# One VectorE order for another in a fused Fourier-filter and SoLU kernel: where two kinds of sums stand in the queue, and how one operand is laid out

## The chip, the cores and the metric

The kernel runs on one core of one Trainium2 chip. The time is device time of that core in microseconds, from one execution of the whole program. Seven executions of the kernel before gave a median of 1732.12 us (1724.58 to 1738.16).

## What is computed

The reference has two parts. The first filters a sequence in the frequency domain: eight examples of 3136 positions by 256 channels, a real Fourier transform along the positions, a product with a complex filter, and the transform back.

```python
X = np.fft.rfft(x, axis=1)
Y = X * (filt_r + 1j * filt_i)[None]
y = np.fft.irfft(Y, n=3136, axis=1)          # (8, 3136, 256)
```

The second takes the 25088 rows of that result through a two-layer block with a softmax-gated unit and a layer norm between the layers.

```python
h = x @ w_in                                  # 256 -> 1024
sm = softmax(h); solu = h * sm
ln = (solu - mean) / sqrt(var + 1e-6) * g_ln
out = ln @ w_out                              # 1024 -> 256
```

Everything is float32.

## The kernel before

**Blocks and pairs.** The 25088 tokens are 196 blocks of 128. A loop `step(k)` runs 205 times; block k's first layer is done in step k, its softmax and normalization in step k+2, its transpose in step k+3, and its second layer some nine steps after its first. Two steps, an even and an odd one, make a pair of blocks. Both layers use Strassen's scheme with seven products on 2x2 halves, so the unit of TensorE work is a pair: seven products of the first layer (line 716, `product(j, m)`, m from 1 to 7, 128x512 outputs) and seven of the second (line 828, `project(p, m)`, four 128x128 matmuls each, which the trace lists as eight instructions). The order of the products is 1, 2, 6, 7 in the even step and 5, 3, 4 in the odd step.

**Who empties the PSUM banks.** ScalarE copies a finished product out with `keep` (line 726) or `keep_out` (line 840, scaled). VectorE adds the later products to what was kept with `finish` (lines 737 and 740, which also find the running minimum for the softmax) and `finish_out` (line 844). Product 7 goes to a bank of its own. `finish(j, k, 1, (k - 1, 1), 2)` reads it, adds the half that was kept after product 5, and only then may product 4 add to the same bank. I call this `finish` the sum of product 7. In the same way project 7 may start only after `finish_out(p, 0, 0, ...)` in the odd step has read project 2, and the even step's `finish_out(p, 1, 0, ...)` needs project 4.

**The steps between.** `exponential` (line 748, ScalarE) and `normalize` (lines 759 to 766) do the softmax: two tiny VectorE instructions, a 128x1024 product with an accumulated mean on VectorE (line 764), and a square on ScalarE (line 766). `turn` (line 774) transposes a block of 128x1024 in 32x32 squares on VectorE. `regroup` (line 786) is the DMA, issued on SP, that brings the transposed squares into place, and `project_sums` (line 695) makes Strassen's sums on GpSimd.

**The Fourier part of the next example runs beside it.** While the blocks of example e are in the two layers, example e+1 or so goes through its transform: loads (line 240, SP), the difference and the sum of two quarters (line 249 VectorE, line 255 GpSimd), first step (line 264 TensorE, line 269 ScalarE), forward products (line 296), filter products (`multiply`, lines 317 to 319, VectorE, one half in the even step and one in the odd step after), the inverse (line 296 and ScalarE line 334). The last stage, the step back, is `back_halves`: 64 small matmuls (line 367) make an even and an odd half in two PSUM banks, ScalarE copies the even half to SBUF (line 371), and `join_halves` (lines 379 and 380, VectorE) adds and subtracts the halves into the tokens `y`, 128x392 elements each. A list `PLAN` gives the step of each piece by hand. The eight pieces of each of examples 2 to 7 fall in even steps; those of example 1 fall in steps 16 to 22, three of them odd and two in step 20.

**Order.** The whole loop is recorded under a manual schedule, so each engine's queue holds its instructions in the order in which `step` emits them, and each engine works its queue in order. Work of the Fourier part hangs in lists by step: `stores` at the start of a step, `products` after the odd step's sum of product 7, `early` behind the exponential, and `late` at the end of the step.

Of the kernel before, what the change touches and what calls it, by code (L numbers as in the profile page):

```python
# [23 lines left out]
N1, N2 = 49, 64  # L24
# [5 lines left out]
NCH = 4  # L30
KD, KF = C // P, DFF // P
PAIR = 2 * S
NT = PAIR // P
LAG = 9
# [60 lines left out]
def kernel(  # L95
# [10 lines left out]
    nc = tc.nc  # L106
# [247 lines left out]
    joins = {}  # L354

    def back_halves(e, ch, pss):

        t4 = t4s.pop((e, ch))
        views = [ps.rearrange("p a c -> p (a c)")[:, 0:KD * NCH * N1].rearrange(
            "p (c i r) -> p c i r", c=KD, i=NCH) for ps in pss]  # L360
        for cb in range(KD):
            for i in range(NCH):
                for g in range(2):
                    rows = slice(64 * g, 64 * g + NK // 2)
                    for h in range(2):
                        c0 = cb * P + 64 * h
                        nc.tensor.matmul(out=views[g][64 * h:64 * h + 64, cb, i, :],  # L367
                                         lhsT=t4[rows, i, c0:c0 + 64], rhs=wb_t[rows],
                                         start=True, stop=True)
        even = t4.rearrange("p i c -> p (i c)")[:, 0:KD * NCH * N1]  # L370
        nc.scalar.copy(out=even, in_=pss[0].rearrange("p a c -> p (a c)")[:, 0:KD * NCH * N1])
        joins[e, ch] = even.rearrange("p (c i r) -> p c i r", c=KD, i=NCH), views[1]

    def join_halves(e, ch):

        even, odd = (v.rearrange("p c i r -> p c r i") for v in joins.pop((e, ch)))
        t0, last = e % 2 * S, N2 // NCH - 1
        to = y[:, :, t0:t0 + S].rearrange("p c (r m j) -> p m c r j", m=N2 // NCH, j=NCH)
        nc.vector.tensor_tensor(out=to[:, ch], in0=even, in1=odd, op=ALU.add)
        nc.vector.tensor_tensor(out=to[:, last - ch], in0=even[:, :, :, ::-1], in1=odd[:, :, :, ::-1],  # L380
                                op=ALU.subtract)
# [14 lines left out]
    with ExitStack() as st:  # L396
# [154 lines left out]
        for n in range(16):  # L551
            (nc.sync, nc.scalar)[n % 2].dma_start(
                out=t2_0[NH * (n % 4):NH * (n % 4) + NH, n // 4, :], in_=rows_x[n:n + 1])
# [6 lines left out]
        for i in range(units):  # L560
# [4 lines left out]
            pss = [ps_t.tile([P, 2, C], FP32, name=f"pc_0_{i}_{u}", tag="t") for u in range(2)]  # L565
# [17 lines left out]
        for i0, n, rows in ((0, 4, P), (4, 4, P), (8, NP - 9, P), (NP - 1, 1, NQ)):  # L583
            f, at = filters[i0]
            nc.sync.dma_start(
                out=f_dram[i0:i0 + n].rearrange("i u q k c -> (u q) i (k c)")[0:rows],
                in_=f[0:rows, at:at + n].rearrange("p i k c -> p i (k c)"))
# [134 lines left out]
    def keep(j, k, i):  # L722

        if k not in hs:
            hs[k] = hpool.tile([P, DFF], FP32, name=f"h_{k}", tag=f"h{k % 2}")
        nc.scalar.copy(out=h_half(k, i), in_=ms[j, 0])  # L726

    def finish(j, k, i, kept, bank):


        if k not in nmaxs:
            nmaxs[k] = small.tile([P, 2], FP32, name=f"nmax_{k}", tag=f"nmax{k % 2}")
            sofar, to = 3.0e38, nmaxs[k][:, 0:1]
        else:
            sofar, to = nmaxs[k][:, 0:1], nmaxs[k][:, 1:2]
        if kept is None:
            nc.vector.tensor_scalar(out=h_half(k, i), in0=ms[j, bank], scalar1=0.0, scalar2=sofar,
                                    op0=ALU.add, op1=ALU.min, accum_out=to)
        else:
            nc.vector.tensor_tensor_reduce(out=h_half(k, i), in0=ms[j, bank], in1=h_half(*kept),  # L740
                                           scale=1.0, scalar=sofar, op0=ALU.add, op1=ALU.min,
                                           accum_out=to)
# [104 lines left out]
    def store_out(p):  # L847
# [7 lines left out]
    blocks = NT * B // 2  # L855

    early, late, stores, loads, products = (
        [[] for _ in range(blocks + LAG + 1)] for _ in range(5))  # L860

    def ahead(t, by):
        return loads[max(0, t - by)]
# [3 lines left out]
    for e in range(1, B):  # L867
        first_at, spectrum_at, back_at = PLAN[e]
        sp = Spectrum(e, pools, load_filter, load_de)
        if e == 1:  # L870
            sp = second
            sp.load, sp.load_de = load_filter, load_de
        for i, t in enumerate(first_at):
            dma = nc.gpsimd.dma_start
            if e == 1:
                if i not in sp.xs:
                    row_loads.append((t, t - 1, -1, lambda sp=sp, i=i, dma=dma: sp.fetch_x(i, [dma] * 2)))
                for u in range(2):
                    (early, late)[u][t].append(lambda sp=sp, i=i, u=u: sp.first(
                        i, (u,), psum(f"pa_{sp.e}_{i}_{u}").rearrange("p a c -> p (a c)").rearrange(  # L880
                            "p (o n) -> p o n", o=1), nc.scalar.copy, sp.xs[i][0:NK, 2 * u:2 * u + 2, :]))
                    (early, late)[u][t].append(lambda sp=sp, i=i, u=u: sp.store_first(
                        i, 2 * u, nc.gpsimd.dma_start))
            else:

                row_loads.append((t, t - 2, -1, lambda sp=sp, i=i: sp.fetch_quarters(i, nc.sync.dma_start)))
                stores[t].append(lambda sp=sp, i=i: sp.difference(i))
                products[t].append(lambda sp=sp, i=i: sp.sum(i))
                late[t].append(lambda sp=sp, i=i: sp.first_quarters(
                    i, [psum(f"pa_{sp.e}_{i}_{g}") for g in range(2)]))  # L890
                stores[t + 1].append(lambda sp=sp, i=i, dma=dma: sp.store_quarters(i, dma))
        for i, t in enumerate(spectrum_at):

            other = e == 1 and i % 2 == 1 and t + 1 < LAG
            add = nc.gpsimd.tensor_tensor if t + 1 < LAG else nc.vector.tensor_tensor


            dma = nc.sync.dma_start if e == 1 else nc.scalar.dma_start
            ahead(t, 2).append(lambda sp=sp, i=i, dma=dma: sp.fetch(i, dma))
            ahead(t, 1 if e == 1 and i % 2 == 1 else 2).append(lambda sp=sp, i=i: sp.fetch_filter(i))  # L900
            ahead(t, 2).append(lambda sp=sp, i=i: sp.fetch_de(i))
            early[t].append(lambda sp=sp, i=i, o=other: sp.forward(i, psum_pair(f"pb_{sp.e}_{i}", o)))
            late[t].append(lambda sp=sp, i=i, add=add: sp.multiply(i, 0, add))
            products[t + 1].append(lambda sp=sp, i=i, add=add: sp.multiply(i, 1, add))
            late[t + 1].append(lambda sp=sp, i=i, o=other: sp.inverse(i, psum_pair(f"pc_{sp.e}_{i}", o)))
            stores[t + 2].append(lambda sp=sp, i=i: sp.store(i, nc.gpsimd.dma_start))


        assert S * (e - 1) <= P * (back_at[0] // 2 * 2) and P * (back_at[-1] + 2) <= S * e // P // 2 * 2 * P
        for ch, t in enumerate(back_at):  # L910
            row_loads.append((
                t, t - 1, spectrum_at[-1] + 2, lambda e=e, ch=ch: fetch_back(e, ch)))
            (late if ch and t == back_at[ch - 1] else early)[t].append(lambda e=e, ch=ch: back_halves(
                e, ch, [psum(f"py_{e}_{ch}_{g}") for g in range(2)]))
            late[t].append(lambda e=e, ch=ch: join_halves(e, ch))
    row_loads.sort(key=lambda load: load[0])
    for n, (t, latest, earliest, load) in enumerate(row_loads):

# [10 lines left out]
    def step(k):  # L929
        j, odd = divmod(k, 2)  # L930
        p = j - (LAG - 1) // 2 if odd else j - (LAG + 1) // 2
        if not 0 <= p < pairs:
            p = None
# [5 lines left out]
        if not odd:  # L939
            if hid:  # L940
                product(j, 1)
                keep(j, k, 0)
            if proj:
                project(p, 5)
                keep_out(p, 1, (0, 1))
            if hid:
                product(j, 2)
        else:
            if hid:
                product(j, 5)  # L950
                keep(j, k - 1, 1)
        if 3 <= k < blocks + 3:
            turn(k - 3)
        if not odd and 0 <= j - 3 < pairs:
            regroup(j - 3, 0)
        if not odd:
            if proj:
                finish_out(p, 1, 1, (0, 1), 1)
            if hid:
                finish(j, k, 0, (k, 0), 1)  # L960
        elif hid:
            finish(j, k, 1, (k - 1, 1), 2)
        for job in products[k]:
            job()
        if 2 <= k < blocks + 2:
# [32 lines left out]
                project(p, 7)  # L998
        if 2 <= k < blocks + 2:
            normalize(k - 2)  # L1000
        if not odd:
            if proj:
                finish_out(p, 1, 0, (1, 0), 1)
                store_out(p)
        else:
            if hid:
                finish(j, k - 1, 1, None, 0)
                finish(j, k, 0, (k, 0), 2)
            if proj:
                keep_out(p, 1, (1, 0))  # L1010
# [39 lines left out]
```

## Time and profile before

| | |
|---|---|
| median of seven executions | 1732.12 us |
| the profiled execution, its own time | 1724.58 us |
| its span of instructions | 1722.8 us |
| TensorE busy | 1577.5 us (92%) |
| VectorE busy | 1298.1 us (75%) |
| GpSimd busy | 1122.8 us (65%) |
| ScalarE busy | 905.8 us (53%) |
| mean granted TensorE clock | 0.982 |

A busy share says how long an engine had an instruction in it, over stages of different kinds. What a change of order is worth is read from the waits: which engine stood idle, before which of its instructions, and whose work ended that idle time. The profile names for each idle stretch the instruction that released it. A line such as `m<-w_in_sb,y` names the tile written and the tiles read; `y` as an operand marks the products that take tokens directly (1, 2 and 4), `s` those that take sums (5, 6, 7 and 3). In timelines the columns are start, duration, engine, line, operation, tiles, shape and count, and in brackets the idle time before and what ended it.

### The profile page before, as it was taken

To read this page: it belongs to the slowest core of one execution; us is meant where nothing else is said; L and a number is where in the kernel's file an instruction comes from. 1 tells how busy PE (TensorE), PEld (TensorE's weight loads), DVE (VectorE), ACT (ScalarE), POOL (GpSimd) and SP (SyncE) were. 2 spreads that over 40 slices of the span, in tenths; PEclk is the share of its full clock that TensorE was granted. 3 is DMA by queue.
4 is the path that set the end of the run, shared out by engine and by line. 5 is a ranking of instruction groups with operands and counts; after the bars stand their busy time and mean duration, and the time that the engine had idled before them with its cause. 6 is when DMAs were issued, how large, how long until landed. Compare 5 with 4: busy or idle time off the path is not lost.

```text
span 1722.8 us, 36835 instructions
## 1 busy us (share of the span) xinstructions
PE 1577.5 (92%) x12710; PEld 1054.5 (61%) x12710; DVE 1298.1 (75%) x2633; ACT 905.8 (53%) x1772; POOL 1122.8 (65%) x1325
## 2 busy tenths in 40 slices
PE   5798789899988999899999998999999999999996
PEld 1353456666656666566656675566665777777776
DVE  1676787887777887787878778786788788777771
ACT  2154454456544555555455654555545656666662
POOL 4444785678666766677567865677655766666663
PEclk8999999999999999999999999999999999999998
DMA  9987888887888788867888778876786666555554
GB/s 254 254 263 212 238 207 208 206 200 178 182 214 216 178 187 220 216 159 167 209 206 202 178 168 214 204 178 162 182 208 146 134 128 126 115 107 107 110 109 91
DMA packets 377805, 312.13 MB, mean 181 GB/s; under 512 B 63322, under 2 KB 343395, under 8 KB 377619
## 3 DMA queue, kind: packets, MB, share of 16 engines
q1 hardware_dynamic: 306260, 169.81, 46.7%
q0 software_dynamic: 34464, 101.68, 20.8%
q10 hardware_dynamic: 36896, 38.28, 8.2%
q8 instruction: 103, 1.69, 0.4%
q14 instruction: 82, 0.67, 0.1%
HBM read 124.86 MB, written 81.50 MB: 120 GB/s over the span
## 4 chain that ended last, share of the span: by engine, by line
PE 54%; DMA 23%; DVE 10%; SPq 4%; POOL 3%; issue 3%; ACT 1%; ACTq 0%; DVEq 0%; POOLq 0%
PE o L828 23%; PE m L716 22%; DMA solu_t<-turn 10%; SPq L786 3%; PE py L367 3%; DMA x<-in_x_dram 2%; DVE turn L774 2%; DMA de<-de_tbl 2%; PE pb L296 2%; PE pa L264 2%; DVE h L764 2%; DMA rows<-rs 1%; PE pc L296 1%; DMA t<-d 1%; DMA out_dram<-ot 1%
## 5 line engine op out<-in xcount | busy, mean ns | idle before, releaser
L766 ACT ACTIVATE e<-h,nmu 128x1024 f32<-128x1024 f32 x196 | 224.8, 1147 | 398.9 <-DVE h L764 398.7
L828 PEld LDWEIGHTS o<-w_out_sb,solu_t 128*128 128x128 f32 x3136 | 384.6, 194 | 60.3 <-issue 37.8
L828 PE MATMUL o<-w_out_sb,solu_t 128*128 128x128 f32 x3136 | 405.3, 278 | 10.2 <-DVE rsum L759 7.4
L828 PEld LDWEIGHTS o<-w_out_sb,u 128*128 128x128 f32 x2352 | 313.2, 195 | 149.7 <-issue 116.9
L716 PE MATMUL m<-w_in_sb,s 128*128 128x512 f32 x784 | 396.3, 607 | 7.8 <-ACT h L726 5.0
L695 POOL TENSOR_TENSOR u<-solu_t 128x512 f32<-128x512 f32 x98 | 140.1, 1430 | 374.1 <-DMA solu_t<-turn 214.3
L716 PE MATMUL m<-w_in_sb,y 128*128 128x512 f32 x588 | 317.4, 623 | 64.4 <-DVE nmax L740 62.1
L828 PE MATMUL o<-w_out_sb,u 128*128 128x128 f32 x2352 | 318.9, 280 | 8.3 <-ACT ot L840 5.8
L844 DVE SCALAR_TENSOR_TENSOR ot<-o,rs_t,ot 128x128 f32<-128x128 f32 x294 | 102.5, 349 | 281.2 <-ACT ot L840 168.2
L764 DVE SCALAR_TENSOR_TENSOR h<-e,rsum,h 128x1024 f32<-128x1024 f32 x196 | 285.8, 1458 | 6.9
L726 ACT COPY h<-m 128x512 f32<-128x512 f32 x294 | 173.5, 590 | 204.2 <-PE m L716 190.8
L774 DVE STREAM_TRANSPOSE turn<-h 128x1024 f32<-128x1024 f32 x196 | 242.4, 1237 | 0.5
L748 ACT ACTIVATE e<-h,nmax 128x1024 f32<-128x1024 f32 x196 | 226.1, 1153 | 0.0
L716 PEld LDWEIGHTS m<-w_in_sb,y 128*128 128x128 f32 x588 | 93.5, 192 | 177.1 <-DVE nmax L740 131.6
L716 PEld LDWEIGHTS m<-w_in_sb,s 128*128 128x128 f32 x784 | 128.5, 191 | 95.7 <-issue 70.4
L840 ACT ACTIVATE ot<-o,rs_t 128x128 f32<-128x128 f32 x392 | 142.5, 363 | 74.2 <-PE o L828 65.9
L695 POOL TENSOR_TENSOR u<-solu_t,u 128x512 f32<-128x512 f32 x98 | 138.7, 1415 | 63.6 <-PE o L828 59.6
L740 DVE CUSTOM_DVE_ANT_0 h<-m,h 128x512 f32<-128x512 f32 x196 | 132.0, 673 | 37.9 <-ACT h L726 22.6
L695 POOL TENSOR_TENSOR u<-u,solu_t 128x512 f32<-128x512 f32 x98 | 139.0, 1419 | 0.6
L695 POOL TENSOR_TENSOR solu_t<-solu_t,solu_t 128x512 f32<-128x512 f32 x98 | 132.6, 1353 | 7.7
L695 POOL TENSOR_TENSOR s<-y 128x128 f32<-128x128 f32 x196 | 102.6, 524 | 1.7 <-DVE y L380 0.7
L367 PEld LDWEIGHTS py<-wb_t,t 50*64 50x64 f32 x3584 | 58.3, 134 | 44.5 <-PE o L828 14.4
(113 smaller groups left out, 1977.5 us busy)
## 6 DMA issues: line engine op xcount, KB each, us to landing
solu_t<-turn SPq DMA_DIRECT2D x784, 128.0 KB
out_dram<-ot SPq DMA_DIRECT2D x196, 128.0 KB
t<-d POOLq DMA_DIRECT2D x112, 200.0 KB, 4.7
d<-x POOLq DMA_DIRECT2D x100, 200.0 KB, 5.9
f<-f_dram POOLq DMA_DIRECT2D x39, 512.0 KB, 8.6
d<-g POOLq DMA_DIRECT2D x39, 512.0 KB, 5.1
t<-d ACTq DMA_DIRECT2D x36, 512.0 KB
x<-in_x_dram SPq DMA_DIRECT2D x112, 98.0 KB
```

The lines of the kernel that those rows point to most:

```text
L367: nc.tensor.matmul(out=views[g][64 * h:64 * h + 64, cb, i, :], lhsT=t4[rows, i, c0:c0 + 64], rhs=wb_t[rows], start=True, stop=True)
L695: nc.gpsimd.tensor_tensor(out=out, in0=in0, in1=in1, op=op)
L716: nc.tensor.matmul(out=ms[j, bank], lhsT=lhsT, rhs=w_in_sb[:, w, :], start=m in (1, 2, 7), stop=True, skip_group_check=True)
L726: nc.scalar.copy(out=h_half(k, i), in_=ms[j, 0])
L740: nc.vector.tensor_tensor_reduce(out=h_half(k, i), in0=ms[j, bank], in1=h_half(*kept), scale=1.0, scalar=sofar, op0=ALU.add, op1=ALU.min, ...
L748: nc.scalar.activation(out=e, in_=hs[k], func=AFT.Exp, bias=nmaxs.pop(k)[:, 1:2], scale=-1.0, accum_out=esum)
L764: nc.vector.scalar_tensor_tensor(out=solu, in0=e, scalar=rsum, in1=solu, op0=ALU.mult, op1=ALU.mult, accum_out=nmu)
L766: nc.scalar.activation(out=e, in_=solu, func=AFT.Square, bias=nmu, scale=-float(DFF), accum_out=variances[g][:, i:i + 1])
L774: nc.vector.transpose(out=turns[g][:, :, i, :], in_=solus.pop(k).rearrange("p (f j) -> p f j", j=32))
L828: nc.tensor.matmul(out=pos[p, bank], lhsT=lhs[:, f, :], rhs=w[:, f, :], start=f == 0 and m in (1, 2, 7), stop=True, skip_group_check=True)
L840: nc.scalar.activation(out=out_half(p, *to)[0], in_=pos[p, 0], func=AFT.Copy, scale=rs)
L844: nc.vector.scalar_tensor_tensor(out=ot, in0=pos[p, bank], scalar=rs, in1=out_half(p, *kept)[0], op0=ALU.mult, op1=ALU.add)
```

## The change

Three edits, all of them to work on VectorE and to one ScalarE copy. Neither the number of instructions of any kind nor the order on TensorE, ScalarE, GpSimd or SP is changed.

1. The joins of the step back move from the end of the step (`late`) to a new list `middle`, which is emitted directly behind `normalize`: ahead of the even step's last `finish_out`, and in an odd step ahead of its two last `finish`. A second step back in the same step (there is one) stays in `late`.
2. In odd steps the sum of product 7 is emitted ahead of `turn` where it was behind it.
3. The even half is written by the ScalarE copy in the order in which the join reads it (channel half, row, position in the group of four). The copy therefore reads PSUM with a step of 49 elements where it read it in sequence, and writes SBUF in sequence as before. The join reads this operand in sequence in its first half, and in reversed groups of four in its second; its other operand, the odd half in PSUM, it reads with the step of 49 elements as before.

```diff
@@ back_halves, join_halves
         even = t4.rearrange("p i c -> p (i c)")[:, 0:KD * NCH * N1]
-        nc.scalar.copy(out=even, in_=pss[0].rearrange("p a c -> p (a c)")[:, 0:KD * NCH * N1])
-        joins[e, ch] = even.rearrange("p (c i r) -> p c i r", c=KD, i=NCH), views[1]
+        even = even.rearrange("p (c r i) -> p c r i", c=KD, i=NCH)
+        nc.scalar.copy(out=even, in_=views[0].rearrange("p c i r -> p c r i"))
+        joins[e, ch] = even, views[1].rearrange("p c i r -> p c r i")
...
-        even, odd = (v.rearrange("p c i r -> p c r i") for v in joins.pop((e, ch)))
+        even, odd = joins.pop((e, ch))
@@ the lists by step
-            (late if ch and t == back_at[ch - 1] else early)[t].append(lambda e=e, ch=ch: back_halves(
+            second_one = ch and t == back_at[ch - 1]
+            (late if second_one else early)[t].append(lambda e=e, ch=ch: back_halves(
                 e, ch, [psum(f"py_{e}_{ch}_{g}") for g in range(2)]))
-            late[t].append(lambda e=e, ch=ch: join_halves(e, ch))
+            (late if second_one else middle)[t].append(lambda e=e, ch=ch: join_halves(e, ch))
@@ step(k)
+        if odd and hid:
+            finish(j, k, 1, (k - 1, 1), 2)
         if 3 <= k < blocks + 3:
             turn(k - 3)
...
-        elif hid:
-            finish(j, k, 1, (k - 1, 1), 2)
         for job in products[k]:
             job()
...
         if 2 <= k < blocks + 2:
             normalize(k - 2)
+        for job in middle[k]:
+            job()
```

More of the change, by code (lines that the diff above doesn't have):

```diff
@@ L855 @@
     blocks = NT * B // 2
-    early, late, stores, loads, products = (
-        [[] for _ in range(blocks + LAG + 1)] for _ in range(5))
+    early, middle, late, stores, loads, products = (
+        [[] for _ in range(blocks + LAG + 1)] for _ in range(6))
     def ahead(t, by):
```

## The prediction, made before the changed kernel ran

> **What bounds the kernel now.** I read the busy shares first, then the list of waits of TensorE, then two stretches of the timeline, then busy time and DMA share by stretch.
>
> ```profile
> PE 1577.5 (92%) x12710; PEld 1054.5 (61%) x12710; DVE 1298.1 (75%) x2633; ACT 905.8 (53%) x1772; POOL 1122.8 (65%) x1325
> ```
>
> TensorE is the fullest, and the idle part of it is what an order can win. Its waits:
>
> ```profile
> PE m L716 <- DVE nmax L740: 62.1, 41, 3.4
> PE pa L221 <- DMA x<-in_x_dram: 9.5, 1, 9.5
> ...
> PE o L828 <- DVE rsum L759: 7.4, 31, 1.0
> PE pa L264 <- POOL x L255: 6.0, 4, 2.2
> PE o L828 <- ACT ot L840: 5.8, 8, 1.5
> ```
>
> One wait stands out: 62.1 us in 41 times. In the order of TensorE's queue every one of them stands before an `m<-w_in_sb,y` behind an `m<-w_in_sb,s`: it is product 4, waiting for the sum of product 7. A heavy pair (step back, filter product and difference in one pair) shows how it arises:
>
> ```profile
> 728.05 0.35 DVE L844 SCALAR_TENSOR_TENSOR ot<-o,rs_t,ot 128x128 f32<-128x128 f32 x1 [2.04 <-PE o L828]
> 728.32 0.82 DVE L379 TENSOR_TENSOR y<-t,py 128x392 f32<-128x392 f32 x1
> ...
> 731.35 1.02 PE L716 MATMUL m<-w_in_sb,s 128*128 128x512 f32 x2
> ...
> 731.70 0.68 DVE L249 TENSOR_TENSOR diff<-x 113x512 f32<-113x512 f32 x1
> 732.30 1.24 DVE L774 STREAM_TRANSPOSE turn<-h 128x1024 f32<-128x1024 f32 x1
> ...
> 733.46 0.65 DVE L740 CUSTOM_DVE_ANT_0 h<-m,h 128x512 f32<-128x512 f32 x1
> ...
> 734.18 1.13 PE L716 MATMUL m<-w_in_sb,y 128*128 128x512 f32 x2 [1.81 <-DVE nmax L740]
> ...
> 736.37 1.16 PE L828 MATMUL o<-w_out_sb,solu_t 128*128 128x128 f32 x8 [0.17 <-DVE rsum L759]
> ```
>
> VectorE idles 2.04 us for project 4, then does 1.46 us of joins (728.32 to 729.78), 1.92 of filter product, 0.60 of difference and 1.16 of transpose before the sum that TensorE has wanted since 732.37. Project 7 then waits again, 0.17 us, for the `finish_out` two places further on.
>
> A light pair, near the end, has no such gap; there VectorE waits for ScalarE:
>
> ```profile
> 1557.01 1.24 DVE L774 STREAM_TRANSPOSE turn<-h 128x1024 f32<-128x1024 f32 x1
> ...
> 1559.08 0.69 DVE L740 CUSTOM_DVE_ANT_0 h<-m,h 128x512 f32<-128x512 f32 x1 [0.83 <-ACT h L726]
> ...
> 1560.47 0.35 DVE L844 SCALAR_TENSOR_TENSOR ot<-o,rs_t,ot 128x128 f32<-128x128 f32 x1 [0.70 <-ACT ot L840]
> ...
> 1563.65 0.35 ACT L840 ACTIVATE ot<-o,rs_t 128x128 f32<-128x128 f32 x1
> ```
>
> **The change part by part.** I took VectorE's instructions from transpose to transpose and sorted the pairs by what lies in them: 16 with join, filter product and difference; 12 with join and filter product; 12 with filter product and difference; 38 light ones (17 with nothing, 17 with a join, 4 with join and difference); 10 with a difference alone; one with a filter product alone; 3 among example 1's odd steps back. The rest lie in the first 220 us or the tail, and are taken as unchanged. In each I moved the instructions as the diff does, with their own start-to-start times.
>
> *Heavy pairs (16).* In the pair above the joins start at 726.02, when the normalization ends, and are over at 727.48, inside the 2.04 us of idle time. The `finish_out` still starts at 728.05. Then 0.27 + 1.92 + 0.60 bring VectorE to 730.84; the kept half is ready at 730.35; the sum runs 0.67 and is done at 731.5. Product 4 starts at 732.37 when TensorE is there: the 1.81 us are gone. But the transpose is only moved, not removed: it ends at 732.65, the second filter product (1.92) at 734.57, and the `finish_out` that project 7 waits for at 734.9 instead of 736.3. TensorE could start project 7 at 734.1, so it waits 0.8 us there. The gain is what left the chain up to that `finish_out`: the joins, 1.46 us. So with this class the removed wait of 34.4 us comes back at project 7 in part: 22 us are won, and not 34.
>
> *The clock.* Six of the heavy gaps, and one of the next class, are followed by 3.41 us at a granted clock of 0.5; all seven follow gaps of 2.08 us or more. At half pace 3.41 us cost 1.7 us of matmul work, some of it hidden in the wait for project 7. Worked out pair by pair it is 6 us more. [...] I take the rows: heavy pairs together -28.
>
> *Join and filter product (12).* The gaps are about 1.2 us, and the same chain through project 7 gives 1.3 us a pair, 0.7 in one, 2.3 in the one with half clock: -16.
>
> *Filter product and difference (12).* No join leaves the chain, and transposing before or after the sum is all one to project 7: 5.6 us of the 6.2 at product 4 come back there, and some pairs lose a little: +1, the one with a filter product alone with them.
>
> *Difference alone (10).* Three have gaps (2.06, 1.60 and 0.55); the difference itself waits for its load. The transpose's 1.16 leaves the way to product 4, and project 7 has room: -3.
>
> *Light pairs (38).* Here the new order is worse. In the pair above the sum cannot start before 1559.08, since ScalarE's copy (line 726) ends at 1559.05. The transpose, which ran while VectorE waited, now follows: 1559.77 to 1560.93, and the `finish_out` starts 0.46 us late. Behind it stand the normalization, the two last sums, and on ScalarE the square and the `keep_out` that ends at 1564.00; the next project 5 starts at 1564.41. Moved by 0.42 to 0.46 plus the hand-over, project 5 slips about 0.09: +3 over 34 pairs, and nothing in the 4 with a difference.
>
> *Odd steps back of example 1 (3).* The join now stands ahead of the two last sums that products 1 and 2 wait for: +1.46 each, against 1.8 won earlier in these pairs: +3.
>
> *Even half in another order.* Rows nearest:
>
> ```profile
> L379 DVE TENSOR_TENSOR y<-t,py x56: 810/819/842, 269.6 to 1483.4; 128x392 f32<-128x392 f32 x56
> L371 ACT COPY t<-py x56: 472/485/486, 265.5 to 1480.3; 128x392 f32<-128x392 f32 x56
> L392 ACT COPY y<-py x16: 846/862/878, 93.9 to 109.4; 128x392 f32<-128x392 f32 x16
> ```
>
> (Minimum, median, maximum in ns.) No row has a ScalarE copy that reads PSUM in steps. The sequential copy is the floor, 485 ns; the copy of line 392, as large but writing in steps, took 862. I take 862, the nearest of its kind, and 1200 as the upper end. ScalarE idles 0.5 us or more between this copy and its next (`keep` waits for product 6), which hides 0.38; at 1200 the next copy is 0.2 late and product 5, some 1.8 us on, doesn't see it. The join took 819; sequential operands (128x512 in 680) would give about 555. [...] At 0.555 it would lie in idle time just the same: 0 us by either.
>
> *Sum.* -28 - 16 + 1 - 3 + 3 + 3 = -40. Against it stands traffic. The transfers are the same in less time:
>
> ```profile
> 636.00:655.00 19.00, 17.22 (x171) 11.34 (x170) 15.67 (x31) 9.45 (x21) 14.71 (x19) 1.00 0.93 225
> 713.20:732.30 19.10, 17.02 (x174) 11.39 (x174) 14.87 (x31) 9.86 (x20) 11.41 (x14) 1.00 0.84 204
> ```
>
> (The last two columns: DMA share, GB/s.) A heavy pair of 19.1 us that becomes 17.6 goes from 0.84 to 0.91; one at 0.93 has no room. The first 100 us show 0.94. Holding the pairs that would exceed it (about five, 1.3 us each) gives back 6. Forecast: -34; 1724.6 becomes 1690.6 in a profiled execution. That execution was the fastest of seven, 7.5 below the median, so from the median 1732.1 it is 1698.
>
> **The rivals.** *All of it and no price for traffic*: -40 to -50, 1682 to 1692 from the median. For it: VectorE idles 0.8 to 2 us in each even step even when full, and late loads show little at TensorE. *The wait moves*: project 7, or loads (GpSimd already waited 214 us for regrouped squares), takes half or more: 1706 to 1722. For it: the middle stretch runs at 0.8 to 0.9 DMA share. Against it: TensorE waited only 2.5 us for GpSimd's sums. *No effect*: all of the heavy gain returns as waits: 1724 to 1741. *Slower*: the odd normalization (line 764) starts 0.45 us later in light pairs and meets GpSimd's sum; at 736.61 it took 2.25 us against its median of 1.285 when a sum had started 0.1 us before it. [...] If all 38 met, +1 us each would cancel the -40; it decides from there, 1735 to 1745 with traffic. Against it: 7 of the 98 odd ones were stretched, and in the light pair GpSimd's sum starts at 1562.11, after 1561.54.
>
> **How the numbers follow.** Likeliest, -26 to -44 (1688 to 1706): 0.56. All of it: 0.12. Half or less: 0.15. No effect: 0.08. Slower: 0.09. Within 0.5% (8.7 us) a measurement of this kernel tells nothing from no change. Faster: 0.83; same 0.08; slower 0.09. The range 1680 to 1728 leaves out some 0.17, nearly all of it above.
>
> **What would show it.** Right: TensorE's wait for line 740 under 8 us; its wait for `rsum` (project 7) up from 7.4 to 25 or more; at most three spells of half clock between 220 and 1650 us of the span, now eight; heavy pairs near 17.6 us; the copy of line 371 near 0.86. Wrong: heavy pairs still near 19 us with new waits on loads, light pairs over 12.5 us, or many odd normalizations over 1.8 us.

## The result, and the profile after

The changed kernel took 1712.24 us (median of 23 executions, 1697.36 to 1727.86) against 1729.14 us for the kernel before (60 executions, those beside later comparisons among them). The ratio is 0.9901, with a 95% interval of 0.9886 to 0.9916: about 17 us faster. The forecast was 34 us faster, 1698 us, range 1680 to 1728. The direction and the range hold; of the gain, half came. The profiled execution of the change was one of its slower ones, 1722.8 us, with a span of 1721.0 us.

From line 372 on, line numbers of the changed kernel are one higher than before: the sum of product 7 is line 741, the transpose 775, the joins 380 and 381, the copy of the even half 372. Busy time first, from the page:

```profile
PE 1588.3 (92%) x12710; PEld 1066.1 (62%) x12710; DVE 1275.6 (74%) x2633; ACT 903.8 (53%) x1772; POOL 1134.5 (66%) x1325
```

VectorE is busy 22.5 us less, though none of its instructions was left out. The joins alone are 29.6 us shorter (112 of them, 0.264 us each, in the row below), so others took some 7 us longer; those in the heavy pairs are told in the part on the prediction. TensorE's waits (who waited, for whom, us in total, times, longest):

```profile
PE o L829 <- DVE rsum L760: 34.0, 35, 1.5
PE m L717 <- ACT h L727: 13.3, 7, 3.8
PE pa L264 <- POOL x L255: 10.5, 8, 2.6
...
PE m L717 <- DVE nmax L741: 6.9, 8, 1.4
PE m L717 <- DVE h L738: 6.3, 10, 1.0
```

The wait of product 4 for the sum of product 7 is down from 62.1 to 6.9 us. The wait of project 7 is up from 7.4 to 34.0, and three waits have grown that the kernel before hardly had: product 3 for ScalarE's copy (5.0 to 13.3 us), the first transform step of the next example for GpSimd's sum of quarters (6.0 to 10.5), and the next pair's products for the last two sums on VectorE (line 738, 1.0 to 6.3). A heavy pair in the timeline of the change:

```profile
732.68 0.55 DVE L380 TENSOR_TENSOR y<-t,py 128x392 f32<-128x392 f32 x1
...
734.75 0.35 DVE L845 SCALAR_TENSOR_TENSOR ot<-o,rs_t,ot 128x128 f32<-128x128 f32 x1 [1.04 <-PE o L829]
...
737.11 0.94 DVE L249 TENSOR_TENSOR diff<-x 113x512 f32<-113x512 f32 x1
737.97 0.68 DVE L741 CUSTOM_DVE_ANT_0 h<-m,h 128x512 f32<-128x512 f32 x1
...
738.91 1.02 PE L717 MATMUL m<-w_in_sb,y 128*128 128x512 f32 x2
...
742.03 1.16 PE L829 MATMUL o<-w_out_sb,solu_t 128*128 128x128 f32 x8 [1.21 <-DVE rsum L760]
```

The joins lie in time that VectorE had idle, product 4 starts without a wait, and project 7 waits 1.21 us. The difference (line 249) takes 0.94 us here, where it took 0.68 before. A light pair:

```profile
1555.79 0.69 DVE L741 CUSTOM_DVE_ANT_0 h<-m,h 128x512 f32<-128x512 f32 x1 [1.98 <-ACT h L727]
...
1556.41 1.24 DVE L775 STREAM_TRANSPOSE turn<-h 128x1024 f32<-128x1024 f32 x1
...
1557.57 0.31 DVE L845 SCALAR_TENSOR_TENSOR ot<-o,rs_t,ot 128x128 f32<-128x128 f32 x1
...
1560.71 0.35 ACT L841 ACTIVATE ot<-o,rs_t 128x128 f32<-128x128 f32 x1
```

VectorE now stands idle for 1.98 us and transposes afterwards, and the `finish_out` no longer has an idle time of its own before it: it is the transpose that it waits for.

The two rows of the even half (min/median/max in ns):

```profile
L380 DVE TENSOR_TENSOR y<-t,py x56: 549/555/564, 275.6 to 1477.7; 128x392 f32<-128x392 f32 x56
L372 ACT COPY t<-py x56: 474/485/524, 273.6 to 1476.5; 128x392 f32<-128x392 f32 x56
```

The ScalarE copy that reads PSUM in steps of 49 elements costs what the sequential one did, 485 ns; the join fell from 819 to 555.

**Where the time went, class by class.** I took the start of the even step's sum (line 740, then 741; the first of three in each pair) as a mark and added up the distances of the marks for pairs of one class. The table gives the difference to the profile before in us; the last column is the difference of the two kernels with less traffic, told below. The forecast's sum is the one before its 6 us for traffic, and its third class counted 13 pairs. All are single profiles, so a few us of any entry can be chance.

| class (pairs) | predicted | change | change again | joins alone | sum alone | layout alone | with less traffic |
|---|---|---|---|---|---|---|---|
| heavy: join, filter product, difference (16) | -28 | -9.7 | -5.1 | -11.1 | -8.5 | -7.0 | -21.4 |
| join and filter product (12) | -16 | -14.8 | -16.7 | -16.8 | -0.9 | -5.4 | -18.1 |
| filter product without join (11) | +1 | +4.4 | +7.9 | +7.5 | +2.2 | +1.1 | -2.3 |
| difference alone (10) | -3 | -0.9 | -2.7 | +3.8 | -3.6 | -2.6 | -1.7 |
| light (38) | +3 | +7.7 | +3.8 | +0.2 | +3.4 | +1.1 | +2.7 |
| odd steps back (3) | +3 | +3.7 | -3.4 | +1.6 | -2.2 | +2.5 | +0.9 |
| sum | -40 | -9.6 | -16.2 | -14.8 | -9.6 | -10.3 | -39.9 |

The pairs without a load of the next example's rows came as predicted. What is missing is missing where a difference is in the pair or next to it. Besides, the first profile of the change reached its first mark at 124.5 us, where the others reach it at 112 to 118, in code that stands ahead of all that was changed.

### The profile page after: what moved, and what is told of

Read it like the earlier page. It is cut to its first block, busy times and chain, and to the rows that moved or that the text cites. A ratio compares the mean times of both kernels' runs of the same rounds, so it can differ in the third digit from the quotient of the medians.

```text
span 1721.0 us, 36871 instructions
## 1 busy us (share of the span) xinstructions
PE 1588.3 (92%) x12710; PEld 1066.1 (62%) x12710; DVE 1275.6 (74%) x2633; ACT 903.8 (53%) x1772; POOL 1134.5 (66%) x1325
## 3 DMA queue, kind: packets, MB, share of 16 engines
q1 hardware_dynamic: 306260, 169.81, 46.7%
## 4 chain that ended last, share of the span: by engine, by line
PE 54%; DMA 26%; DVE 8%; POOL 5%; issue 4%; SPq 2%; ACT 1%; ACTq 0%; DVEq 0%; POOLq 0%
PE m L717 22%; PE o L829 22%; DMA solu_t<-turn 12%; DMA x<-in_x_dram 4%; PE py L367 3%; DVE h L765 2%; PE pb L296 2%; PE py L390 2%; PE pa L264 2%; DMA out_dram<-ot 2%; DMA d<-x 1%; DMA t<-d 1%; DMA de<-de_tbl 1%; DVE turn L775 1%; SPq L787 1%
## 5 line engine op out<-in xcount | busy, mean ns | idle before, releaser
L696 POOL TENSOR_TENSOR u<-solu_t 128x512 f32<-128x512 f32 x98 | 148.9, 1520 | 395.6 <-DMA solu_t<-turn 248.8
L717 PE MATMUL m<-w_in_sb,s 128*128 128x512 f32 x784 | 396.1, 607 | 13.3 <-ACT h L727 13.3
L829 PEld LDWEIGHTS o<-w_out_sb,u 128*128 128x128 f32 x2352 | 308.7, 194 | 158.1 <-issue 105.0
L696 POOL TENSOR_TENSOR u<-solu_t,u 128x512 f32<-128x512 f32 x98 | 144.1, 1470 | 46.5 <-PE o L829 41.6
L717 PEld LDWEIGHTS m<-w_in_sb,y 128*128 128x128 f32 x588 | 97.7, 195 | 118.6 <-DVE nmax L741 45.7
L696 POOL TENSOR_TENSOR solu_t<-solu_t,solu_t 128x512 f32<-128x512 f32 x98 | 134.5, 1373 | 7.7
L696 POOL TENSOR_TENSOR u<-u,solu_t 128x512 f32<-128x512 f32 x98 | 134.3, 1370 | 0.6
L696 POOL TENSOR_TENSOR s<-y 128x128 f32<-128x128 f32 x196 | 107.0, 546 | 5.8 <-ACT y L393 4.8
```

Of the source, the lines that this page charges most:

```text
L696: nc.gpsimd.tensor_tensor(out=out, in0=in0, in1=in1, op=op)
L717: nc.tensor.matmul(out=ms[j, bank], lhsT=lhsT, rhs=w_in_sb[:, w, :], start=m in (1, 2, 7), stop=True, skip_group_check=True)
L829: nc.tensor.matmul(out=pos[p, bank], lhsT=lhs[:, f, :], rhs=w[:, f, :], start=f == 0 and m in (1, 2, 7), stop=True, skip_group_check=True)
```

## The experiments

My theory after the result: the chain up to the `finish_out` ahead of project 7 sets the gain, so the joins carry it; and what is missing was taken back by transfers that land late, with queues in order behind them. The rivals: the place of the sum of product 7 decides; or the losses are engine work that the sums left out.

**The change again**, for a second profile.

> The changed kernel once more, for a second profile beside the kernel before on the same chip. The first gave 0.990 (1712 against 1729 us); its profiled execution was 12 us late already at the first pair of blocks, in code that the change doesn't touch. Theory (the chain through project 7, with late loads taking back the rest): ratio 0.988 to 0.992; the first pair at 112 to 125 us, by chance; light pairs +0.09 us each, pairs with join and filter product -1.1 to -1.5 each, and against them three to six single losses of 1 to 6 us, at other pairs than in the first profile, before a wait on a load. Rival (the losses are built into the new order): the same losses at the same pairs again.

Measured: 1711.35 against 1727.03 us, 0.9907 (0.9881 to 0.9933). Its first mark lies at 113.3 us, so the 12 us of the first profile were of that execution. The light pairs that are free of other trouble show +0.09 us each again, those with join and filter product mostly -0.9 to -1.9. The large single losses lie partly at other pairs: of the first profile's losses of +5.56, +4.39, +2.56 and +3.77 us, the second has -0.06, +1.56, -0.61 and +4.14 at the same places. So one comes back whole and one in part, and the others move. Five pairs of the second profile past the first 220 us lose more than 1 us, within the three to six expected.

**The joins alone.**

```diff
-            late[t].append(lambda e=e, ch=ch: join_halves(e, ch))
+            (late if second_one else middle)[t].append(lambda e=e, ch=ch: join_halves(e, ch))
```

> Only the joins moved (edit 1). Theory: the gain of a heavy pair is what leaves the chain up to the finish_out before project 7, and that is the joins alone; the product 4 gaps shrink from about 2.1 to 0.7 us, and project 7 follows them: nearly the whole gain of the change, ratio 0.988 to 0.993. Light pairs at +0.00 each, since the sum stays behind the transpose. Rival (the wait of product 4 for the sum of product 7 is the thing, and the sum's place decides it): a third of the gain at most, 0.996 or more.

Measured: 1711.63 us, 0.9915 (0.9893 to 0.9938): the change's own gain, within the intervals. TensorE's waits:

```profile
PE m L716 <- DVE nmax L740: 28.3, 31, 2.2
PE pa L264 <- POOL x L255: 15.0, 11, 1.8
PE m L716 <- ACT h L726: 11.7, 9, 4.4
PE o L828 <- DVE rsum L759: 10.3, 34, 1.0
```

Product 4 still waits 28.3 us for the sum, and it makes no difference: where it no longer waits, project 7 does. Light pairs are at +0.00.

**The sum of product 7 alone.**

```diff
+        if odd and hid:
+            finish(j, k, 1, (k - 1, 1), 2)
         if 3 <= k < blocks + 3:
             turn(k - 3)
...
-        elif hid:
-            finish(j, k, 1, (k - 1, 1), 2)
```

> Only the sum of product 7 ahead of the transpose (edit 2). Theory: product 4's wait falls by 1.16 us a pair, and comes back whole before project 7; light pairs lose 0.09 us each, 34 of them: ratio 0.996 to 1.001, TensorE's wait for line 740's sum down to about 20 us and that before project 7 up to about 45. Rival (the sum's place decides): 0.989 to 0.993.

Measured: 1725.97 us, 0.9997 (0.9976 to 1.0017): nothing.

```profile
PE o L828 <- DVE rsum L759: 46.8, 36, 1.7
PE m L716 <- DVE nmax L740: 19.1, 24, 1.3
```

The two waits together are 65.9 us; before they were 69.5. This is the clearest row of the study: 43 us were taken from the longest wait of the bounding engine, and 39.4 of them stood again two products further on in its queue. The place of the sum doesn't decide; that rival is out.

**The layout alone.**

```diff
-        nc.scalar.copy(out=even, in_=pss[0].rearrange("p a c -> p (a c)")[:, 0:KD * NCH * N1])
+        nc.scalar.copy(out=even, in_=views[0].rearrange("p c i r -> p c r i"))
```

> Only the even half in reading order (edit 3). The profile of the change shows the joins at 0.55 us instead of 0.82 and the ScalarE copy unchanged at 0.48. With the joins still in the chain this takes 0.53 us from every pair that has a join and a filter product: 28 x 0.53 = 15 us by the chain, about half of it after late loads: ratio 0.993 to 0.997. Rival (the product 4 gaps are set elsewhere): 0.998 to 1.002.

Measured: 1718.43 us, 0.9949 (0.9927 to 0.9970), with the joins at 0.55 us. By itself it is worth half of the change, since the joins are then still in the chain; behind the normalization they are covered, and shortening them adds little (0.9901 for the whole change, 0.9915 for the joins moved alone, intervals overlapping). Edits 1 and 3 draw on the same time.

**The sum's place by step.** It stands ahead of the transpose only where the odd step has a difference or a filter product.

```diff
-        if odd and hid:
+        ahead_of_turn = odd and hid and (products[k] or stores[k])
+        if ahead_of_turn:
             finish(j, k, 1, (k - 1, 1), 2)
...
+        elif hid and not ahead_of_turn:
+            finish(j, k, 1, (k - 1, 1), 2)
```

> The change, but the sum of product 7 stands ahead of the transpose only in odd steps that have a difference or a filter product; in the others it is behind it, as before. Theory: the light pairs lose the 0.09 us that each showed, 34 x 0.09 = 3 us better than the change: ratio 0.987 to 0.991, and the last 25 pairs at 12.26 and 13.54 us again. Rival: something else in the light pairs holds them, and they stay at +0.09.

Measured: 1708.03 us, 0.9883 (0.9856 to 0.9910). The pairs with neither join nor filter product nor difference are back at 208.4 us in sum, as before, against 210.0 in the change. 3 us is what was forecast, though the intervals overlap.

**Less traffic, under both orders.** From example 3 on half of each filter and table load is left out (its first half serves for both), and half of each output row isn't stored.

```diff
-            out=f[0:rows, 0:pairs],
-            in_=f_dram[i:i + pairs].rearrange("i u q k c -> (u q) i (k c)")[0:rows])
+            out=f[0:rows, 0:pairs].rearrange("p i k c -> p i (k c)")[:, :, 0:256 if sp.e > 2 else 512],
+            in_=f_dram[i:i + pairs].rearrange("i u q k c -> (u q) i (k c)")[
+                0:rows, :, 0:256 if sp.e > 2 else 512])
...
-            nc.sync.dma_start(out=rows[2 * second + i], in_=ots[p][:, i, :])
+            nc.sync.dma_start(out=rows[2 * second + i][:, :, 0:P], in_=ots[p][:, i, 0:P])
```

> The kernel before with less traffic: from example 3 on only the first half of each filter load and of each table load is fetched (and that half is used for both), and only the first half of each output row is stored, so that a heavy pair moves some 0.5 MB of 3.9 less. Theory: the gaps before product 4 are made by VectorE's queue and not by loads: 0.994 to 1.000.

> The changed kernel with the same traffic left out. Theory (late loads, with GpSimd and ScalarE in order behind them, took back what was missing): the change gains more here than with all its traffic, 25 us or more against the kernel before with less traffic; ratio to the kernel before 0.978 to 0.985. Rival (the missing half is a chain of engine work in the pairs with a difference, GpSimd's own instructions above all): the gain stays at 15 to 20 us, and TensorE still waits 10 us or more for GpSimd's sum of quarters.

Measured: the kernel before 1713.16 us, 0.9907 (0.9888 to 0.9927), which my 0.994 missed: it, too, lost some 15 us to its traffic, mostly in pairs with a difference. The changed kernel 1678.06 us, 0.9706 (0.9684 to 0.9728), more than was expected. Between the two the change is worth 35.1 us, twice as much as with all the traffic, and the classes sum to -39.9 (last column of the table). TensorE's waits in the changed kernel with less traffic:

```profile
PE o L832 <- DVE rsum L763: 32.1, 36, 1.7
...
PE pa L264 <- POOL x L255: 5.1, 5, 2.3
...
PE m L720 <- DVE nmax L744: 4.2, 5, 1.5
...
PE m L720 <- ACT h L730: 0.6, 2, 0.4
```

The wait that the forecast named, project 7's, stays at 32.1. The two that it didn't name go from 13.3 to 0.6 and from 10.5 to 5.1. Both lead back to transfers, seen through queues in order. ScalarE's copy stood behind its own load issues for 17.1 us in the first profile of the change and 5.2 in the second, and the lists of the kernel before and of the two with less traffic don't have this wait. GpSimd's wait for the regrouped squares stands ahead of the sum of quarters in its queue: it is 214.3 us before, 248.8 and 279.3 in the change, and 197.8 in the change with less traffic (L696 and L699 are one line).

```profile
ACT h L727 <- issue: 17.1, 4, 6.1
POOL u L696 <- DMA solu_t<-turn: 248.8, 71, 11.1
POOL u L699 <- DMA solu_t<-turn: 197.8, 65, 6.7
```

A late copy in the timeline of the change with all its traffic (ACTq is ScalarE's sequencer, issuing):

```profile
1101.77 0.19 ACT L767 ACTIVATION_READ_ACCUMULATOR e<-h,nmu 128x1 f32 x1
1105.26 0.37 ACTq L286 DMA_DIRECT2D t<-d  x1
1106.40 1.56 ACTq L677 DMA_DIRECT2D de<-de_tbl  x1
1108.01 0.58 ACT L727 COPY h<-m 128x512 f32<-128x512 f32 x1 [6.05 <-issue]
...
1108.65 2.08 PE L717 MATMUL m<-w_in_sb,s 128*128 128x512 f32 x2 [3.83 <-ACT h L727]
```

ScalarE is free from 1101.96 on, but the next things in its queue are two loads, and these aren't issued until 1105.26 and 1106.40. The trace's semaphore events show why: the last landing on the semaphore that the first issue waits for is at 1105.18, on that of the second at 1106.38. The copy of product 5 stands behind them, and TensorE for 3.83 us behind the copy; from 1107.07 on its granted clock is 0.5 for 6.83 us. The wait counts as ScalarE's in the list, and no ScalarE instruction was slow. VectorE has the same in the difference: its waits for the loads of x are 5.0 us in the kernel before and 12.7 and 9.4 in the two profiles of the change, and with less traffic no wait of the difference for a load is left under either order.

**GpSimd's order.** The sum of quarters ahead of the next pair's small sums.

```diff
-                products[t].append(lambda sp=sp, i=i: sp.sum(i))
+                stores[t].append(lambda sp=sp, i=i: sp.sum(i))
...
-        if odd and j + 1 < pairs:
-            pair_sums(j + 1)
         for job in stores[k]:
             job()
+        if odd and j + 1 < pairs:
+            pair_sums(j + 1)
```

> The changed kernel with GpSimd's sum of quarters (line 255) ahead of the four small sums of the next pair, where it stood behind them. In the second profile of the change it began 1.1 to 7 us after the difference that it needs, in a queue without gaps, and TensorE waited 13.9 us for it. Theory (GpSimd's queue is the new wait): that wait falls under 5 us, and the time by 4 to 9 us against the change: ratio 0.985 to 0.989. Rival (late loads decide, or the small sums are now late themselves): within 2 us of the change, 0.989 to 0.992.

What it acts on, in the second profile of the change:

```profile
659.18 1.92 POOL L696 TENSOR_TENSOR u<-solu_t 128x512 f32<-128x512 f32 x1 [8.87 <-DMA x<-in_x_dram]
...
669.54 0.47 POOL L696 TENSOR_TENSOR s<-y 128x128 f32<-128x128 f32 x1
...
672.24 1.27 POOL L255 TENSOR_TENSOR x<-x 113x512 f32<-113x512 f32 x1
...
673.56 0.65 PE L264 MATMUL pa<-x,wq_t 49*64 49x512 f32 x2 [1.75 <-POOL x L255]
```

The difference that this sum reads had ended at 665.25, 7.0 us before the sum began; between the two GpSimd did two sums of 128x512, an issue of a filter load and the next pair's four small sums, the first of which is the second line. Its queue was late besides: by the first line it had stood idle for 8.87 us until a transfer landed.

Measured: 1703.55 us, 0.9859 (0.9827 to 0.9891), and the wait for the sum of quarters at 0.4 us. Product 3's wait for ScalarE stays (17.1 us). To see whether that reserve was opened by the change, the kernel before got the same edit:

> The kernel before with GpSimd's sum of quarters ahead of the next pair's small sums, the edit that took 8 us off the changed kernel. Theory (the wait for GpSimd became one only when VectorE's order stopped hiding it): the kernel before shows 6 us of that wait, in pairs with a difference alone, and none in heavy pairs, so 0 to 5 us at most: ratio 0.997 to 1.001. Rival (the edit is worth the same under either order): 0.994 to 0.996.

Measured: 1719.19 against 1726.66 us, 0.9950 (0.9933 to 0.9967). The rival is right: the edit takes 7 to 9 us under either order. So GpSimd's order isn't what the change was missing: with it in both kernels the change is worth 0.9950 less 0.9859, some 16 us, no more than without it. In the heavy pairs of the kernel before TensorE never waited for this sum, and yet they got 6.8 us shorter in that profile. Of these, 2.3 us are VectorE's differences and filter sums (lines 249 and 319), which took 37.0 us there in place of 39.3. The rest isn't shown; I leave it open.

**Together, and the loads moved.**

> The changed kernel with three mends: the sum of product 7 ahead of the transpose only where a difference or a filter product follows, GpSimd's sum of quarters ahead of the next pair's small sums, and the three odd steps' joins of example 1 left at the end of the step. Theory: the first two add, since one is in light pairs and the other in pairs with a difference: 3 and 8 us better than the change; the third 0 to 4 us: ratio to the kernel before 0.980 to 0.986. Rival (they draw on the same reserve, late loads): no better than the GpSimd order alone, 0.985 to 0.988.

The edits are those of the two experiments above, and

```diff
-            (late if second_one else middle)[t].append(lambda e=e, ch=ch: join_halves(e, ch))
+            (late if second_one or t % 2 else middle)[t].append(lambda e=e, ch=ch: join_halves(e, ch))
```

Measured: 1703.65 against 1731.32 us, 0.9847 (0.9812 to 0.9883). It is faster than both kernels, but not told apart from GpSimd's order alone (0.9859).

```diff
-            dma = nc.sync.dma_start if e == 1 else nc.scalar.dma_start
+            dma = nc.sync.dma_start
...
-        nc.scalar.dma_start(out=de[:, 0:pairs],
+        nc.sync.dma_start(out=de[:, 0:pairs],
```

> As the kernel with the three mends, and the loads that ScalarE issues in the loop (rows for the forward product, and tables) are issued from SP. In the changed kernel ScalarE stood up to 6 us at these two issues while its copy for product 5 waited behind them, and TensorE waited 8 to 17 us for that copy. Theory (ScalarE's own issues hold it): that wait falls under 3 us, and the time by 4 to 10 us against the three mends. Rival (the transfers themselves are late, and SP has its own queue to hold up): the wait moves to TensorE's forward product or to GpSimd's wait for the regrouped squares, and the time is the same or worse by up to 10 us.

Measured: 1771.99 us, 1.0232 (1.0193 to 1.0271), 68 us slower than with ScalarE's issues, where neither theory nor rival had allowed more than 10. The wait for ScalarE's copy did fall, to 1.6 us. In its place:

```profile
PE pb L296 <- DMA de<-de_tbl: 85.7, 35, 6.7
```

On SP these loads stand behind the regrouping DMAs and the waits of those (for TensorE alone 183.0 us, against 96.0 without the move), and land too late for the forward product. ScalarE's queue, for all its 14.7 us, was the better place.

## Why the prediction was right in sign and twice too large

*What bounds the kernel.* Right. The wait of product 4 was 62.1 us and is 6.9 (7.9 in the second profile), under the 8 that I named as the sign.

*Heavy pairs, the chain through project 7.* Right, and the main point: the removed wait comes back there as far as the transpose goes. I put that wait at 25 us or more, 34.0 and 34.7 were measured, and the sum alone (0.9997) shows that the chain and not the longest wait is what counts. With less traffic thirteen of the sixteen heavy pairs take 17.87 to 18.41 us and three 18.88 to 18.99, where I looked for 17.6; with all the traffic they take 17.92 to 23.49 in the two profiles. The class gives -21.4 of the -28 with less traffic.

*VectorE's own times.* This term I put at nothing: I moved instructions with their own durations. The differences and the filter sums of line 319 in the heavy pairs, 48 instructions that each read two SBUF operands, take 39.3 us in the profile before and 41.6 and 46.7 in the two of the change; with less traffic 36.1 and 40.5. Those of over 0.8 us are 17 before, 22 and 25 in the change, and each of them had a GpSimd instruction beside it; of those that had none (46 in all pairs before, 27 in the first profile of the change), none took more than 0.70. I had looked for this in the odd normalization alone. With less traffic it is 4.4 us, of the 6.6 that the class lacks there; whether all of it lies on the chain isn't shown.

*The clock.* The seven spells at half clock behind gaps of product 4 are gone, but between 220 and 1650 us six are left in the first profile of the change and four in the second, where I allowed three, now behind the new waits (3.07, 2.47, 2.63 and 1.75 us among them). The last is shorter than any gap that half clock followed in the profile before (2.08 us the shortest), and the length of a gap alone doesn't tell: of the two gaps of 2.35 us in the profile before, one was followed by half clock and one wasn't. With less traffic there are three spells.

*Join and filter product.* Right: -16 forecast, -14.8 and -16.7.

*Light pairs.* Right to the hundredth in the pairs that nothing else disturbs: +0.09. Most of the rest of that class's +3.8 to +7.7 is one pair, +4.39 and +1.56 us, in which ScalarE's copy stood 4.70 and 2.59 us behind its two load issues and product 3 waited for it.

*Traffic.* This is the step that failed. I let the share of DMA time rise to 0.94 and charged 6 us for the pairs that would exceed it. Measured against the class sums, -40 became -9.6 and -16.2: the term is some 24 us by the second profile, and by the medians 18 (35.1 with less traffic, 16.9 with all). That the sum with less traffic is again 40 is in part luck, since the heavy class gave 6.6 less and others gave more. The share didn't tell where the cost began. Two pairs of the second profile of the change, from sum to sum:

```profile
839.21:855.70 16.49, 16.10 (x172) 11.07 (x174) 14.62 (x29) 8.89 (x19) 8.85 (x12) 1.00 0.99 225
1088.95:1112.44 23.49, 18.48 (x173) 12.34 (x168) 16.53 (x31) 10.27 (x21) 13.55 (x17) 0.93 0.77 192
```

(The last three: clock, DMA share, GB/s.) The first has join and filter product, ran at a share of 0.99, and gained its 1.31 us in full. The second is the heavy pair whose loss came back, +4.14 us; it has 0.77, and the mean over a longer stretch tells as little: between 640 and 740 us the share was 0.85 before, 0.88 in the change and 0.80 with less traffic.

What the transfers cost here is read from when they landed, as with the two loads at 1105.18 and 1106.38 us above. Each load has its place in a queue and a consumer that comes up in order. My reading: when the pairs got shorter (by 1.2 us on average where join and filter product are), consumers that had just been served came too early, and with them what stands behind them on VectorE (12.7 us of waits for x, 5.0 before), GpSimd (248.8 for regrouped squares, 214.3 before) and ScalarE (17.1 behind its load issues, none before). That less traffic gives the gain back is shown; how the 18 us divide among these ways isn't. The profile before showed it in small: 5.0 us of the difference waiting for x, GpSimd 214.3 us for regrouped squares, and loads on ScalarE's queue that took up to 2.8 us to issue. I had named the first two, but priced them by TensorE's own list, where they were hidden behind product 4. The measured 1712 lies in the range of a rival, "the wait moves" (1706 to 1722), to which I gave 0.15, and the loads that it named are what the runs show.

*The layout.* The price of the copy was wrong: it took 0.485 us, as before, and not 0.86. The nearest row (line 392, 0.862) differs in writing SBUF in steps; whether that is what it pays for, no run tried. ScalarE's read of PSUM in steps of 49 elements ran as fast as its sequential one, and the join, whose PSUM operand is still read in steps, took 0.555 us, as the sequential rows had led me to estimate, where it took 0.819 before. What was saved came from its SBUF operand: with that alone in reading order (the layout alone) the join took 0.552. Why steps in that operand cost 264 ns and in the one in PSUM next to nothing wasn't shown. For the sum it made no difference, as I argued, because behind the normalization the joins are covered.

*The slower rival.* The odd normalizations that were stretched over 1.7 us are 7 of 98 in the change, 7 before: as I named it, it didn't happen. In the heavy pairs VectorE's differences and filter sums did take longer, 2.3 and 7.4 us in sum, those of over 0.8 us all beside a GpSimd instruction, as told above.

## What to carry to other kernels

Before counting a removed wait, walk the queue of the engine that made it wait to the next instruction that the bounding engine needs, and count only the work that leaves the chain up to there: here the joins, not the moved transpose. Don't take the durations of moved instructions as given: look at what the other engines do in the time to which they go. Then ask what was hidden behind the wait. In this kernel, with its loads timed by hand, the faster pairs met their transfers earlier, and it showed on the engines whose queues held a wait for a load or an issue in front of work that the bounding engine needed (in the first profile ScalarE's copy stood 17.1 us behind its issues, and VectorE's difference waited 12.7 us for its rows); list such places from the profile before (idle time of each engine that ends in a transfer, and loads on a compute engine's queue), and price them by how late they would be, not by the share of DMA time. A run with less traffic tells how much of a missing gain they hold.

## What the runs showed of the hardware that I had not expected

Reading PSUM in steps of 49 four-byte elements cost ScalarE nothing here (485 ns for 128x392, as in sequence), and VectorE (555 ns) next to nothing: by its rows with sequential operands in the kernel before, 405 ns for 256 elements a partition (line 317) and 680 for 512 (line 318), 392 would take some 551, which is an estimate. One SBUF operand in the same steps cost VectorE 264 ns a join (819 with it, 555 without). And gaps of 1.75 us on TensorE in the first profile of the change, and of 1.63, 1.75 and 1.75 in the second, were followed by 3.41 us at half clock. Each of the four had a gap of 1.0 us some 4 us ahead of it; one more gap of 1.75 us that had this too was not followed.
